# A routed-attention and gated-MLP kernel: a second chunk goes to the 26-product out-projection, and the forms it needs are made earlier

## The chip, the cores and the metric

The kernel runs on one core of a Trainium2 chip. The metric is the device time of one execution in microseconds (us). Each time is one run of the whole program; the kernel before has three.

## What is computed

```python
# routed attention, B=4, H=8, S=768, D=64, 16 centroids per head
mask = q_assign[:, :, :, None] == k_assign[:, :, None, :]
scores = np.where(mask, scale * np.matmul(q, k.transpose(0, 1, 3, 2)), -1e9)
attn_out = np.matmul(softmax(scores), v)
# its heads side by side are x: 3072 tokens x 512
h = x @ w_in                      # 512 -> 2048
g = h * erf(softplus(h))
out = g @ w_out                   # 2048 -> 512
```

All of it is float32. The change concerns only the last product, `g @ w_out`, and what is made for it.

## The kernel before

The attention takes the first 405 us or so and is not touched. Then the 3072 tokens go through the MLP in six chunks of 512 (`NCHUNK`). The 2048 hidden features are two lots of 1024.

**In-projection** (`hidden`, line 727). One call makes one lot of one chunk. It works in four steps of `j`, and in each step multiplies by Strassen's scheme in Winograd's form: seven products of half-size blocks in place of eight. One product there is two matmuls of 128x128 by 128x256; the profile records every float32 matmul as two. A product lands in one of eight PSUM banks (`bank`, line 676, in turn), and VectorE adds it to the results (`fresh`, line 686; ScalarE copies the first of the seven). TensorE can run ahead of these additions until all eight banks are taken.

**Gate** (`gate`, line 741; `gate26`, line 868). ScalarE computes Softplus and Erf, each behind a table load, and VectorE multiplies the outcome into `g`.

**Out-projection.** There are two kinds. Chunks 0 and 1 use `project` (line 779): seven products for each lot and each half of the chunk, so 28 products of four matmuls, 112 matmuls. Chunks 2 to 5 use `project26` (line 921): one scheme of 26 products of four matmuls, 104 matmuls, for both lots at once. The tables `RIGHT`, `LEFT`, `LEFT_STEPS` and `AFTER` (lines 64 to 107) say which sums of `w_out` blocks (right forms) and of `g` blocks (left forms) each product takes, and how VectorE and ScalarE spread the products over the outputs.

**The right forms of the 26-product scheme.** `forms26` (line 832) makes them on GpSimd, once, from the blocks of `w_out`; these lie in memory in the form that `project` uses, so part of that is first turned back. Each step of `FORM_STEPS` (line 55) adds or subtracts two blocks of 128x1024 in two pieces of 128x512. Eight forms stay in SBUF: `slot` (line 812) gives six places in `more_out`, by `HOME`, and two in `w_out`. Ten forms stream: they are stored to DRAM (`b_dram`) and read back in turn into a ring of three buffers (`load_stream`, line 853). Before, 14 pieces are made beside chunk 1's second `project` (line 1260) and 26 beside chunk 2's in-projections (line 1268, through `paired`, line 899); a b12 block of `w_out` that chunk 1's `project` still multiplies by can't be turned back until it has.

**What sets the order.** Instructions on TensorE, VectorE, ScalarE and GpSimd stand in the order in which the Python code issues them (`InOrder`, line 113). Work that belongs to another stage is put in a list, `aside_work`, and `block` (line 708) issues `pace` items of it after each product. The DMAs of the sync engine (SP) are one queue that waits in order. The main loop is at lines 1238 to 1278. The order around the change is:

| stage | before | after |
|---|---|---|
| 1 | chunk 1 in-projection, lot 0 | the same |
| 2 | chunk 0 `project`, lot 1 | the same |
| 3 | chunk 1 in-projection, lot 1 | the same, with the form pieces |
| 4 | chunk 1 `project`, lot 0, then lot 1 | chunk 1 `project26` |
| 5 | chunk 2 in-projections, then `project26` | the same |

All recorded instructions carry line 121 in the profile, that of the helper in `InOrder`, so they are told apart by their tiles. `g`, `osb`, `u` and `x_own` are what they are in the code; `g_more` is the buffer of the left forms in chunks 0 and 1 and the ring after that; `bank` and `turned` are PSUM.

Of the kernel before, what the change touches and what calls it, by code (L numbers as in the profile page):

```python
# [3 lines left out]

# [6 lines left out]
F32 = mybir.dt.float32  # L11
# [9 lines left out]
P = 128  # L21
# [30 lines left out]
FIRST_MASKS = {(2, 0): ("k", 0), (2, 1): ("q", 0), (2, 2): ("k", 1), (5, 2): ("q", 1)}  # L52

KAPPA = {1: (0, 1), 2: (0, 0), 0: (1, 1), 3: (1, 0)}
FORM_STEPS = [
    (0, -2, -8, 1, -1), (10, -4, -8, -1, 7), (9, -5, -6, -1, 3), (1, -3, -5, -1, -1), (2, -6, 1, 1, -1),
    (9, -4, 2, -1, 0), (9, -7, 1, -1, 5), (6, -1, -5, 1, 1), (3, -6, 10, -1, -1), (4, 10, 6, -1, -1),
    (9, 1, 0, -1, 4), (7, -7, -8, -1, 8), (6, -6, 6, -1, -1), (9, -2, 6, 1, 2), (10, -7, 10, 1, 6),
    (5, -7, 0, -1, -1), (9, -1, 5, 1, 9), (7, -3, 10, -1, -1),
]  # L60
EARLY_FORMS = (2, 3, 4, 5, 6, 7)
HOME = (1, 0, 2, 3, 4, 5)
LAG = 1
RIGHT = [
    2, 7, -3, 100, -6, 3, 101, 4, -1, 102, 6, 103, 0,
# [42 lines left out]
DONE = {0: 15, 6: 20, 7: 23, 1: 23, 5: 23, 3: 24, 4: 25, 2: 25}  # L108
N_STREAM = 10
RING = 3  # L110


class InOrder:
# [16 lines left out]
def kernel(  # L130
# [671 lines left out]


    ring, extra = [], []
    b_dram = dram.tile([N_STREAM, P, FG * HM], F32, name="b_dram")

    def w_block(b):
        lot, h = KAPPA[b // 2]
# [9 lines left out]
    def flat(t):  # L818
        return t.rearrange("p f m -> p (f m)")
# [7 lines left out]
            else:  # L827
                extra.append([t[:, i * HM : (i + 1) * HM] for i in range(3)])

    turns26 = itertools.cycle((9, 8))  # L830

    def forms26(early):
        work = []
        for f in (0, 2) if early else (4, 6):
            b12, b22 = w_out[:, f : f + 2, HM:], w_out[:, HF + f : HF + f + 2, HM:]
            work.append(functools.partial(minus_of, b12, b22, b12, ge))
        for n, (o, a, b, sign, k) in enumerate(FORM_STEPS):
            if (n in EARLY_FORMS) != early:
                continue
            o = next(turns26) if o == 9 else o  # L840
            out_, a_, b_ = (slot(x) if x >= 0 else w_block(-1 - x) for x in (o, a, b))
            form = plus_of if sign > 0 else minus_of

            def piece(f, out_=out_, a_=a_, b_=b_, form=form, k=k):
                c = slice(f, f + 2)
                form(out_[:, c], a_[:, c], b_[:, c], ge)
                if f and k >= 0:
                    nc.sync.dma_start(out=b_dram[k].rearrange("p (f m) -> p f m", f=FG), in_=out_)

            work += [functools.partial(piece, f) for f in (0, 2)]  # L850
        return work

    def load_stream(k):
        nc.sync.dma_start(out=flat(ring[k % RING]), in_=b_dram[k % N_STREAM])

    def left26(n, i):
        if i >= 16:
# [37 lines left out]
    def hidden26(n, lot, generation=()):  # L895
        generation = list(generation)
        first_steps = [functools.partial(left_step, n, x) for x, step in enumerate(LEFT_STEPS) if step[0] < 0]

        def paired(work):
            if not generation:  # L900
                return work
            both = []
            for w in work + idle(14 - len(work)):
                g = generation[:1]
                del generation[:1]
                both.append(lambda w=w, g=g: [f() for f in (w, *g)])
            return both

        def middle():
            finish_aside()  # L910
            aside_work.extend(paired(gate_work(n, lot, 0, first_steps if lot else ())))

        if lot:
            aside_work.extend(paired(gate_work(n, 0, 1)))
        else:
            aside_work.extend(paired([]))
        hidden(n, lot, {1: middle})
        finish_aside()
        return generation

    def project26(n):
        for s in range(2):
            osb_of[n, s] = outp.tile([P, 2, DM], F32, name="osb")
        temps = extra[3]

        def c_at(i):
            if i >= 8:
                return temps[i - 8]
            t = i // 2
            return osb_of[n, t // 2][:, t % 2, (i % 2) * HM : (i % 2 + 1) * HM]  # L930

        first_half, second_half, gate_products = gate26(n, 1, 1)
        curves = {-1: first_half[0], 0: first_half[1], 1: second_half[0], 2: second_half[1]}
        gate_products = [gate_products[i] for i in (3, 1, 0, 2)]
        between = right_forms(ve, *x_parts(n + 1)) if n + 1 < NCHUNK else []
        banks26 = {}

        def evict(p):
            m = banks26.pop(p)
            for op, d, src, sign in AFTER[p]:  # L940
                dst = c_at(d)
                source = m if op in "ca" else c_at(src)
                if op in "aA":
                    (plus_of if sign > 0 else minus_of)(dst, dst, source)
                elif op == "C" and p == 4:
                    if sign > 0:
                        ve.tensor_copy(out=dst, in_=source)
                    else:
                        ve.tensor_scalar(out=dst, in0=source, scalar1=-1.0, scalar2=None, op0=ALU.mult)
                elif sign > 0:  # L950
                    ae.copy(out=dst, in_=source)
                else:
                    ae.activation(out=dst, in_=source, func=ACT.Copy, scale=-1.0)
            for t in range(4):
                parts = [DONE[2 * t], DONE[2 * t + 1]]
                o = osb_of[n, t // 2]
                if n + 1 < NCHUNK:
                    if max(parts) == p:
                        nc.sync.dma_start(out=out_v[2 * n + t // 2, :, t % 2], in_=o[:, t % 2])
                else:  # L960
                    for v in range(2):
                        if parts[v] == p:
                            c = slice(v * HM, (v + 1) * HM)
                            nc.sync.dma_start(out=out_v[2 * n + t // 2, :, t % 2, c], in_=o[:, t % 2, c])

        curves[-1]()
        for p, r in enumerate(RIGHT):
            banks26[p] = m = bank()
            lhs = left26(n, LEFT[p])
            g26 = N_STREAM * (n - 2) + r - 100  # L970
            rhs = ring[g26 % RING] if r >= 100 else slot(r) if r >= 0 else w_block(-1 - r)
            for f in range(FG):
                te.matmul(m, lhsT=lhs[:, f], rhs=rhs[:, f], start=(f == 0), stop=(f == FG - 1))
            if r >= 100:
                if g26 + RING < N_STREAM * (NCHUNK - 2):
                    load_stream(g26 + RING)
            for x, step in enumerate(LEFT_STEPS):
                if step[0] == p:
                    left_step(n, x)
            if p < 3:  # L980
                evict(p)
                curves[p]()
            elif p - LAG >= 3:
                evict(p - LAG)
            if p in (4, 5):
                for f in gate_products[(p - 4) * 2 : (p - 4) * 2 + 2]:
                    f()
            if p >= len(RIGHT) - 4 and between:
                between.pop(0)()
            if p == 12:  # L990
                load_x(n + 2)
        for p in sorted(banks26):
            evict(p)
        for s in range(2):
            for lot in range(2):
                del g_of[n, s, lot]
# [244 lines left out]
    aside_work += together(idle(2) + gates(0, 0, (0,)), all_weights(4, N_LATE))  # L1241
    hidden(0, 1, pace=2, first=ve.tensor_copy)
    finish_aside()
    for n in range(2):
        between = right_forms(ve, *x_parts(n + 1)) if n + 1 < NCHUNK else []
        if n == 0:
            aside_work += gates(0, 0, (1,), between) + gates(0, 1, (0,))
        else:
            aside_work += gates(n, 1, (0, 1), between)
        project(n, 0, 2 if n else 3)  # L1250
        finish_aside()
        if n == 0:
            aside_work += together(gates(0, 1, (1,)), idle(2) + [fence] + out_forms[2] + out_forms[3])
            hidden(1, 0, first=ve.tensor_copy)
            finish_aside()
            load_x(2)
            aside_work += gates(1, 0)
        if n == 1:
            take_places(2)
            aside_work += forms26(True)  # L1260
        project(n, 1, 2)
        finish_aside()
        if n == 0:
            hidden(1, 1)
            finish_aside()
            load_x(3)
    take_places(2)
    generation = forms26(False)
    for n in range(2, NCHUNK):
        generation = hidden26(n, 0, generation)  # L1270
        generation = hidden26(n, 1, generation)
        for work in generation:
            work()
        generation = []
        if n == 2:
            for k in range(RING):
                load_stream(k)
        project26(n)


# [30 lines left out]
```

## Time and profile before

| | |
|---|---|
| time, median of 3 runs | 984.88 us (984.54 to 985.0) |
| the profiled execution, its own time | 984.51 us |
| its span from first to last instruction | 982.8 us |
| granted TensorE clock over the span | 0.999 |
| TensorE busy | 971.8 us |
| VectorE busy | 748.5 us |
| GpSimd busy | 404.9 us |
| stores of right forms to DRAM (`b_dram<-g_more`), issue to landing | 2.6 us |
| reads of right forms (`g_more<-b_dram`), issue to landing | 3.3 us |

The profiled execution is 0.37 us shorter than the median, so a difference worked out in the profile is taken off the median as it is. The span leaves out 1.7 us that lie around it. "Busy" of an instruction includes what it waits for after it was handed to its engine, for example for a memory port.

### The profile page before, as it was taken

What the parts mean: (1) busy time and instruction counts of PE and PEld (TensorE: products, weight loads), DVE (VectorE), ACT (ScalarE), POOL (GpSimd) and SP (SyncE); (2) the same over time, 40 slices, a digit from 0 to 9 for tenths busy, and PEclk for the clock granted to TensorE, in tenths of its full rate; (3) what the DMA queues carried; (4) which work ended last, traced back from release to release, by engine and by line L of the source; (5) the groups of instructions that cost most, each with busy time, mean ns of one, the idle gap of its engine ahead of it and who ended that gap; (6) DMA issues with size and microseconds to landing.
All of it is one profiled execution on the core that took longest, in us unless ns stands there. A gap on an engine that the chain in (4) does not pass through costs nothing.

```text
span 982.8 us, 20793 instructions
## 1 busy us (share of the span) xinstructions
PE 971.8 (99%) x8298; PEld 726.6 (74%) x8298; DVE 748.5 (76%) x1417; ACT 518.9 (53%) x771; POOL 404.9 (41%) x277
## 2 busy tenths in 40 slices
PE   8999999999999999999999999999999999999998
PEld 3555555555555555688888888887888888888887
DVE  8888888888888886879767586668666866685766
ACT  3777777777777665486523320552166226413541
POOL 1688887787888888762210079500000000000000
PEclk9999999999999999999999999999999999999999
DMA  9444444444444210232001103413302420141023
GB/s 215 89 110 110 110 109 109 109 109 102 96 109 111 51 35 18 92 105 87 1 0 43 43 26 144 153 65 109 128 0 80 135 86 1 56 138 64 1 86 107
DMA packets 155696, 82.12 MB, mean 84 GB/s; under 512 B 129488, under 2 KB 139728, under 8 KB 155600
## 3 DMA queue, kind: packets, MB, share of 16 engines
q1 hardware_dynamic: 153248, 80.50, 30.2%
q8 instruction: 65, 1.06, 0.5%
q10 hardware_dynamic: 2352, 0.30, 0.2%
q14 instruction: 31, 0.25, 0.1%
HBM read 62.95 MB, written 17.83 MB: 82 GB/s over the span
## 4 chain that ended last, share of the span: by engine, by line
PE 93%; DVE 3%; ACT 2%; issue 1%; DMA 0%; DVEq 0%; ACTq 0%
PE bank L121 40%; PE turned L121 31%; PE sc L121 16%; PE wide L121 6%; ACT a_s L121 1%; DVE g L121 1%; DVE nmx L121 1%; ACT L121 1%; DMA in_q<-in_q_dram 0%; DVE kT L121 0%; DVE g_more L121 0%; DVE sims L121 0%; DVE osb L121 0%; DVE qT L121 0%; ACT osb L121 0%
## 5 line engine op out<-in xcount | busy, mean ns | idle before, releaser
L121 POOL TENSOR_TENSOR more_out<-more_out,pr 128x768 f32<-128x768 f32 x128 | 217.1, 1696 | 18.7 <-ACT pr L121 10.1
L121 DVE TENSOR_REDUCE nmx<-wide 128x2 f32<-128x768 f32 x189 | 180.5, 955 | 48.2 <-PE wide L121 47.2
L121 ACT ACTIVATE pr<-sc 128x768 f32<-128x768 f32 x192 | 148.9, 812 | 94.2 <-PE wide L121 78.6
L121 PE MATMUL turned<-pr,in_v 128*32 128x194 f32 x3072 | 145.5, 330 | 0.0
L121 DVE TENSOR_TENSOR g<-bank,g 128x256 f32<-128x256 f32 x222 | 89.6, 420 | 60.3 <-PE bank L121 36.9
L121 PEld LDWEIGHTS turned<-pr,in_v 128*32 128x32 f32 x3072 | 91.5, 109 | 51.2 <-issue 21.3
L121 PE MATMUL bank<-x_own,w_in 128*128 128x256 f32 x424 | 104.5, 380 | 0.0
L121 PE MATMUL sc<-qT,kT 64*128 64x384 f32 x528 | 98.3, 486 | 0.0
L121 DVE TENSOR_TENSOR g<-g 128x512 f32<-128x512 f32 x96 | 66.8, 696 | 30.7 <-PE bank L121 20.9
L121 PEld LDWEIGHTS bank<-x_own,w_in 128*128 128x128 f32 x424 | 80.3, 190 | 11.6 <-issue 0.6
L121 ACT ACT_TABLE_LOAD x48 | 61.6, 1283 | 44.6 <-DVE g L121 43.9
L121 PE MATMUL bank<-w_out,g 128*128 128x256 f32 x352 | 81.2, 379 | 0.0
L121 DVE TENSOR_TENSOR g<-a_s,g 128x512 f32<-128x512 f32 x96 | 72.2, 769 | 5.4 <-ACT a_s L121 5.4
L121 PE MATMUL bank<-x_more,more_in 128*128 128x256 f32 x296 | 76.0, 379 | 0.0
L121 PEld LDWEIGHTS bank<-w_out,g 128*128 128x128 f32 x352 | 66.9, 190 | 9.1
L121 POOL TENSOR_TENSOR more_out<-pr,pr 128x768 f32<-128x768 f32 x32 | 60.2, 1882 | 27.9 <-ACT pr L121 27.9
L121 PEld LDWEIGHTS <-qv 64*128 64x128 bf16 x384 | 27.0, 93 | 52.8 <-issue 36.6
L121 PEld LDWEIGHTS sc<-qT,kT 64*128 64x128 f32 x528 | 50.0, 187 | 21.2 <-ACT inv L121 2.3
L121 PE MATMUL wide<-kv,qv 64*128 64x384 bf16 x378 | 64.1, 328 | 1.3 <-DVE nmx L121 0.6
L121 PE MATMUL wide<-km,qm 64*128 64x384 bf16 (+1 forms) x378 | 62.6, 327 | 0.0
L121 PEld LDWEIGHTS bank<-x_more,more_in 128*128 128x128 f32 x296 | 56.2, 190 | 7.7
L121 ACT COPY g<-bank 128x256 f32<-128x256 f32 x28 | 10.2, 365 | 92.2 <-PE bank L121 87.4
(195 smaller groups left out, 1790.0 us busy)
## 6 DMA issues: line engine op xcount, KB each, us to landing
g_more<-b_dram SPq DMA_DIRECT2D x40, 512.0 KB, 3.3
x_own<-in_moe_w_in_dram SPq DMA_DIRECT2D x13, 512.0 KB, 4.4
in_v<-in_v_dram SPq DMA_DIRECT2D x32, 192.0 KB, 3.1
x_dram<-more_out SPq DMA_DIRECT2D x128, 48.0 KB, 2.0
x_own<-x_dram SPq DMA_DIRECT2D x6, 1024.0 KB, 5.2
in_k<-in_k_dram SPq DMA_DIRECT2D x59, 96.0 KB, 2.8
in_q<-in_q_dram SPq DMA_DIRECT2D x58, 96.0 KB, 2.8
out_dram<-osb SPq DMA_DIRECT2D x20, 256.0 KB, 2.7
```

What stands on the lines that cost most here:

```text
L121: ins = getattr(self.engine, name)(*args, **kw)
```

## The change

Chunk 1 goes through `hidden26` (its lot 1) and `project26` as chunks 2 to 5 do. So `forms26` has to be finished one and a half stages earlier, while chunk 0's second `project` still uses `w_out` and `more_out` in their old form. The 18 steps and two turnings become 20 steps in two tables, again 40 pieces of 128x512. The 24 pieces of `EARLY_FORMS` touch only places that chunk 0's lot 0 has left; the 16 of `LATE_FORMS` write places of lot 1. `HOME` is permuted for this. A form that an in-place turning would have given is held in a spare buffer (`HELD`, the ends of two ring tiles). Two resident forms, slots 0 and 5, go to DRAM and are read back once their places are free (`KEPT`, `load_kept`). Two of the first three streamed forms are already in their ring buffers, so only one is read before `project26` (`load_stream(1)`, after the last piece). The gates of chunk 1's lot 0 are both issued beside chunk 0's second `project`, whose `pace` goes from 2 to 3, and no left forms of Strassen's kind are made for chunk 1. The load of chunk 3's `x` and the right forms of chunk 2's `x` move into chunk 1's `project26`.

```diff
-HOME = (1, 0, 2, 3, 4, 5)
+EARLY_FORMS = [
+    (-6, -4, -6, -1, None), (11, -2, -8, -1, None), (1, -3, -5, -1, None), (2, -6, 1, 1, None),
+    (0, -4, 11, -1, 7), (8, -7, 11, -1, 8), (9, -5, -6, -1, 3), (11, -2, 11, 1, 10),
+    (8, -7, 11, -1, 11), (6, -1, -5, 1, 1), (9, -1, 8, 1, 9), (8, 1, 11, -1, 4),
+]
+LATE_FORMS = [
+    (3, -6, 0, -1, None), (4, 0, 6, -1, None), (0, -7, 0, 1, 6), (7, -3, 0, -1, None),
+    (10, -4, 2, -1, 0), (6, -6, 6, -1, None), (9, -2, 6, 1, 2), (8, -7, 1, -1, 5),
+]
+HOME = (4, 0, 2, 3, 1, 5)
+KEPT = {0: 10, 5: 11}
+HELD = 11
...
+    def place26(x, f):
+        if x == HELD:
+            return extra[f // 2].rearrange("p j t -> p (j t)").rearrange("p (f m) -> p f m", f=2)
+        return (slot(x) if x >= 0 else w_block(-1 - x))[:, f : f + 2]
...
+    def load_kept(i):
+        nc.sync.dma_start(out=slot(i), in_=b_dram[KEPT[i]].rearrange("p (f m) -> p f m", f=FG))
...
-        nc.sync.dma_start(out=flat(ring[k % RING]), in_=b_dram[k % N_STREAM])
+        nc.sync.dma_start(out=flat(ring[(k + 2) % RING]), in_=b_dram[k % N_STREAM])
...
-    for n in range(2):
...
-        if n == 1:
-            take_places(2)
-            aside_work += forms26(True)
-        project(n, 1, 2)
...
-    generation = forms26(False)
-    for n in range(2, NCHUNK):
...
+    aside_work += together(gates(0, 1, (1,)), idle(2) + [fence] + out_forms[2] + out_forms[3])
+    take_places(2)
+    hidden(1, 0, first=ve.tensor_copy)
+    finish_aside()
+    load_x(2)
+    making = forms26(EARLY_FORMS)
+    for work in making[:8]:
+        work()
+    del making[:8]
+    aside_work += together(gate_work(1, 0, 0) + gate_work(1, 0, 1), making)
+    project(0, 1, 3)
+    finish_aside()
+    take_places(2)
+    making = forms26(LATE_FORMS)
+    making.insert(2, functools.partial(load_kept, 5))
+    making.append(functools.partial(load_kept, 0))
+    making.append(functools.partial(load_stream, 1))
+    for n in range(1, NCHUNK):
+        if n > 1:
+            hidden26(n, 0)
+        hidden26(n, 1, making if n == 1 else ())
+        project26(n)
```

## The prediction

> **What bounds the kernel now.** First the page: busy shares, and the chain that ended last by engine.
>
> ```profile
> PE 971.8 (99%) x8298; PEld 726.6 (74%) x8298; DVE 748.5 (76%) x1417; ACT 518.9 (53%) x771; POOL 404.9 (41%) x277
> PE 93%; DVE 3%; ACT 2%; issue 1%; DMA 0%; DVEq 0%; ACTq 0%
> ```
>
> TensorE is the bound, so a matmul less is time less, unless TensorE stops somewhere. In the chain in order of time, 10.36 us of TensorE hold 48 matmul records: 0.2158 each, so 0.4316 for one float32 matmul. Where it stops is read from stages. TensorE's timeline gives their borders; the table of windows gives busy time and records by engine, in the order TensorE, weight loads, VectorE, ScalarE, GpSimd.
>
> ```profile
> 602.20:626.40 24.20, 24.20 (x113) 21.29 (x113) 12.66 (x25) 7.95 (x10) 24.20 (x21) 1.00 0.34 131
> 626.40:651.10 24.70, 24.62 (x114) 21.01 (x113) 17.99 (x37) 13.80 (x15) 2.36 (x2) 1.00 0.25 86
> 651.10:698.70 47.60, 45.36 (x209) 39.35 (x208) 37.88 (x79) 15.65 (x32) 0.00 (x0) 1.00 0.39 128
> 698.70:722.90 24.20, 24.20 (x114) 21.30 (x113) 13.65 (x34) 7.95 (x10) 0.00 (x0) 1.00 0.16 55
> 722.90:747.05 24.15, 24.15 (x113) 21.26 (x112) 16.97 (x41) 14.41 (x16) 0.00 (x0) 1.00 0.00 1
> 747.05:791.95 44.90, 44.90 (x210) 39.52 (x208) 34.28 (x72) 15.14 (x30) 0.00 (x0) 1.00 0.42 135
> ```
>
> The first three lines are chunk 2's two in-projections and its 26 products, the others chunk 3's. 104 matmuls are 104 x 0.4316 = 44.89 us, and chunk 3 needs no more; chunk 2 takes 47.62, 2.73 over. Its in-projections take 48.86 where 112 matmuls are 48.34: 0.52 over. All other stages from 408 us on are at their number, and about 4.2 us follow the last matmul. The only 3.25 us that TensorE loses are in chunk 2, the one with GpSimd beside it. VectorE's timeline shows why (start, us, operation):
>
> ```profile
> 578.02 2.77 DVE L121 TENSOR_TENSOR g<-a_s,g 128x512 f32<-128x512 f32 x2
> 581.04 1.42 DVE L121 TENSOR_TENSOR g_more<-g 128x512 f32<-128x512 f32 x1
> ...
> 623.54 5.76 DVE L121 TENSOR_TENSOR g<-a_s,g 128x512 f32<-128x512 f32 x1
> ...
> 629.56 0.68 DVE L121 TENSOR_TENSOR g<-a_s,g 128x512 f32<-128x512 f32 x1
> ```
>
> And GpSimd's:
>
> ```profile
> 578.52 3.39 POOL L121 TENSOR_TENSOR more_out<-w_out 128x512 f32<-128x512 f32 x2
> ...
> 623.80 2.50 POOL L121 TENSOR_TENSOR g_more<-w_out,more_out 128x512 f32<-128x512 f32 x2
> 626.25 2.51 POOL L121 TENSOR_TENSOR w_out<-w_out,g_more 128x512 f32<-128x512 f32 x2
> ```
>
> A VectorE addition from SBUF alone takes 0.68 us free and on average 1.38 beside GpSimd (nine from 573.35 to 585.74), while additions from PSUM stay at 0.42. GpSimd's pieces follow each other 1.23 us apart when free and 1.68 when VectorE comes between. One VectorE operation, at 623.54, waited through four pieces until GpSimd had none left. VectorE then never caught up within the stage: ScalarE's table load ahead of the products starts 5.74 us into chunk 2's product stage (656.83) and 1.37 into chunk 3's (748.42). Of these 4.37 us of lag TensorE lost 2.73: 1.64 are free.
>
> **What the Trainium skill says.** "SBUF — State Buffer", section Who interferes with whom: a VectorE instruction with two SBUF inputs shares a read port with a GpSimd instruction that reads SBUF; the second to issue waits for the first. The trace agrees with 1.38 against 0.68, and PSUM additions untouched. It differs at 623.54, where the wait outlasted several GpSimd instructions. "ScalarE: Activation LUTs", section What ACT_TABLE_LOAD costs: about 1283 ns; the trace has 1283 in the mean.
>
> **The change part by part.** *Fewer products.* The order of TensorE's instructions has 8 matmuls less: 112 become 104. 8 x 0.4316 = **-3.45**.
>
> *Chunk 2 loses its company.* No GpSimd piece is left after chunk 1, so chunk 2 runs as chunk 3 does: **-3.25**, unless chunk 1 hands a lag on.
>
> *GpSimd's 40 pieces move.* The last old form ends at 494.40 (493.12 + 1.28), and the early 24 follow at once; their places are free since 481. They meet 8 VectorE operations at the end of chunk 1's lot 0, and 8 gate products and 6 half-size additions beside chunk 0's second `project`: 24 x 1.23 + 16 x 0.45 + 6 x 0.22 = 38.0, to 532.4. By then the late pieces' places are free (that `project` ends at 529.7). Late: 16 x 1.23 + 7 x 0.45 = 22.9, to **555.3**. Chunk 1's 26 products start at 529.7 + 24.17 = 553.9, each 1.73 long. The last form is used as product 13; the one on the longest way is stream 1 for product 6: after the last piece its buffer is stored (2.6) and read anew (3.3), to 561.3, and product 6 starts at 553.9 + 6 x 1.726 = 564.3. Margin 3.0, so nothing; were every piece contended, 494.4 + 40 x 1.68 = 561.6, and 3.3 late.
>
> *VectorE beside them, up to 529.7.* Its 8 operations in chunk 1's lot 0 cost 8 x 0.70 = 5.6 more in a window of 12.0 us where it was busy 9.75: some 3.4 late, and eight banks let TensorE run seven products (6.0 us) ahead: nothing. Beside `project` the contention costs 8 x 0.70 + 6 x 0.6 = 9.2, and eight Strassen sums of 0.6 no longer needed give back 4.8; seven products are 12.1 us ahead there. At the end the second gate's products wait for ScalarE: first products done about 522.5, two loads and four curves of 1.05 make 529.3, four contended products 5.5 and the additions between them about 1: VectorE reaches the next stage at 536. TensorE needs its second bank again at 537.5. Bounds 0 to 1.5 (products at 1.75, as the worst of 575.68); I take **+0.3**. A gain is excluded: TensorE loses nothing there now.
>
> *Chunk 1's lot 1 and products.* Late pieces meet three left forms (about 544, absorbed: VectorE needs 17 of 24 us) and four gate products within the last 4.4 us, which can't be: 4 x 0.70 = 2.8. The gate's table load then comes 1.37 + 2.8 = 4.2 into the product stage; less 1.37 and the free 1.64: **+1.2**. Bounds: 0 if the pieces have thinned out; 7 x 0.70 - 1.64 = 3.3 if nothing is absorbed.
>
> *DMAs and SP.* Two stores and two reads of kept forms are added and two ring reads drop out, on SP, which waits in order: chunk 0's last two output stores now stand behind form stores and the read into slot 5, till about 540. Who needs them is `osb`, reused at 555; nothing waits. The load of chunk 3's x moves to about 575 and is used after 690. Both cost nothing; if a store came 15 us later, that would show at once.
>
> Sum: -3.45 - 3.25 + 0.3 + 1.2 = -5.2. The profiled execution, 984.51 (span 982.8, and 1.7 around it), becomes 979.3; the median, 0.37 above it, 984.88 - 5.2 = **979.7**.
>
> **The rivals.** *The stall only moves* (0.18): chunk 1 pays what chunk 2 paid, 3.25, so 984.88 - 3.45 = 981.4, up to 982.9. For it: the same pieces meet the same kind of gate products. Against: the 5.76 us wait came once among some sixteen meetings.
>
> *Forms late* (0.10): contended throughout, stream 1 is 3.3 late, with the other terms 979.7 + 3.3 = 983.0. Against: GpSimd took 1.23 wherever VectorE was on PSUM.
>
> *GpSimd keeps the port* (0.20, slower): the wait at 623.54 followed 18 free pieces and ended with GpSimd's work. In chunk 1's lot 0 VectorE's first meeting, at 496.6, comes after ten free pieces (from 484.28), with some 22 ahead and no wait for TensorE until about 523.9 (494.4 + 24 x 1.23). Frozen so long, 27.3, less the 6.0 ahead, TensorE loses 21.3: 984.88 - 5.2 + 21.3 = 1001. It decides from 5.2 + 6.0 = 11.2 us of freezing, nine pieces. Against: in fifteen other meetings VectorE got in after at most one piece.
>
> That the matmuls don't get fewer is excluded by the instructions' order.
>
> **How the numbers follow.** Forecast 979.7, chance 0.52, its own range 978.2 (no stall at all: 984.88 - 6.7) to 981.5. Range 978.0 to 984.0: with it come the moved stall and late forms; about 0.2 is left out, the slow case. A measurement of this kernel tells 0.2% (2 us) from no change: faster means under 982.9. Forecast, moved stall and a part of late forms: 0.70; within 0.11; slower 0.19.
>
> **What would show it.** Right: chunks 2 to 5 each 48.3 and 44.9; chunk 1's products 45 to 48; GpSimd done near 555 with no gap over 1 us; VectorE's SBUF additions 1.0 to 1.8 from 496 to 553, none over 3. Wrong: one over 10 us, TensorE idle on a ring buffer at product 6, or a product stage of chunk 1 over 49.

## The result and the profile after

The median went from 984.90 us (six runs, 984.54 to 985.00) to **978.82 us** (six runs, 978.31 to 979.01): 6.08 us less, ratio 0.9938 with a 95% interval of 0.9925 to 0.9951. The forecast was 979.7. The profiled execution took 978.7, with a span of 976.8.

The first two lines of the page after, busy shares and the chain of waits by engine (the helper that issues all instructions is at line 124 in the kernel after and its variants):

```profile
PE 968.1 (99%) x8282; PEld 724.4 (74%) x8282; DVE 757.9 (78%) x1431; ACT 526.8 (54%) x799; POOL 409.9 (42%) x277
PE 97%; DVE 1%; SPq 1%; issue 0%; DMA 0%; ACT 0%; DVEq 0%
```

TensorE has 16 records less, which is 8 float32 matmuls. Its share of the chain rose from 93 to 97%: what it used to wait for is gone. The table of windows, with borders from TensorE's timeline (TensorE busy, weight loads, VectorE, ScalarE and GpSimd, each with its records; then granted clock, DMA share, GB/s): chunk 1's second in-projection, its 26 products, chunk 2's two in-projections, its 26 products.

```profile
530.05:554.22 24.17, 24.17 (x113) 21.28 (x112) 21.27 (x34) 8.81 (x11) 24.04 (x17) 1.00 0.43 157
554.22:599.16 44.94, 44.94 (x209) 39.44 (x208) 35.92 (x75) 15.04 (x30) 0.00 (x0) 1.00 0.51 170
599.16:623.33 24.17, 24.17 (x113) 21.28 (x112) 13.63 (x34) 7.95 (x10) 0.00 (x0) 1.00 0.17 54
623.33:647.51 24.18, 24.18 (x114) 21.28 (x112) 17.00 (x41) 14.41 (x16) 0.00 (x0) 1.00 0.00 1
647.51:692.40 44.89, 44.89 (x209) 39.52 (x208) 34.27 (x72) 15.13 (x30) 0.00 (x0) 1.00 0.42 135
```

The 47.62 us of chunk 2's products are now 44.89, and its in-projections 48.35 instead of 48.86: it runs as chunk 3 does. Chunk 1's products, which now have GpSimd's work ahead of them, take 44.94, 0.05 over the number of their matmuls. All 40 of GpSimd's pieces lie between 494.70 and 554.09, one directly after the other: from the end of chunk 1's first in-projection, beside chunk 0's second `project`, to the end of the second in-projection.

VectorE's timeline shows its additions from SBUF among those pieces (start, us, operation):

```profile
496.92 0.82 DVE L124 TENSOR_TENSOR g<-a_s,g 128x512 f32<-128x512 f32 x1
498.98 1.66 DVE L124 TENSOR_TENSOR g<-a_s,g 128x512 f32<-128x512 f32 x1
...
551.37 1.59 DVE L124 TENSOR_TENSOR g<-a_s,g 128x512 f32<-128x512 f32 x1
...
553.22 1.42 DVE L124 TENSOR_TENSOR g<-a_s,g 128x512 f32<-128x512 f32 x1
...
555.22 0.67 DVE L124 TENSOR_TENSOR g<-a_s,g 128x512 f32<-128x512 f32 x1
...
556.15 0.67 DVE L124 TENSOR_TENSOR g<-a_s,g 128x512 f32<-128x512 f32 x1
```

No operation comes near the 5.76 us of before: from 496 to 554 they took 0.68 to 1.76 us. Of the second gate's four products two were contended; the other two fell after GpSimd's last piece and took 0.67. GpSimd's timeline has that last pair of pieces:

```profile
548.22 2.96 POOL L124 TENSOR_TENSOR g_more<-w_out 128x512 f32<-128x512 f32 x2
551.15 2.94 POOL L124 TENSOR_TENSOR g_more<-w_out,more_out 128x512 f32<-128x512 f32 x2
```

ScalarE's timeline has the table load that measures VectorE's lag, 3.02 us into the product stage (557.24 - 554.22), where chunk 2 of before had 5.74:

```profile
557.24 1.28 ACT L124 ACT_TABLE_LOAD   x1 [6.77 <-DVE g L124]
```

And the chain of waits in order of time stays on TensorE across product 6, which starts at about 564.6; stream 1 had landed at 560.50:

```profile
556.11 3.45 PE turned L124 x16
559.57 10.36 PE bank L124 x48
569.93 3.50 PE turned L124 x16
```

### The profile page after: what moved, and what is told of

It reads as the page before. It is cut to its first block, busy times and chain, and to the rows that moved or that the text cites. A ratio compares the mean times of both kernels' runs of the same rounds, so it can differ in the third digit from the quotient of the medians.

```text
span 976.8 us, 20838 instructions
## 1 busy us (share of the span) xinstructions
PE 968.1 (99%) x8282; PEld 724.4 (74%) x8282; DVE 757.9 (78%) x1431; ACT 526.8 (54%) x799; POOL 409.9 (42%) x277
## 4 chain that ended last, share of the span: by engine, by line
PE 97%; DVE 1%; SPq 1%; issue 0%; DMA 0%; ACT 0%; DVEq 0%
PE bank L124 43%; PE turned L124 31%; PE sc L124 17%; PE wide L124 6%; SPq L124 1%; DVE nmx L124 1%; DMA in_q<-in_q_dram 0%; DVE kT L124 0%; DVE qT L124 0%; DVE km L124 0%; DVE turned L124 0%; DVE sims L124 0%; ACT qm L124 0%; DVE g_more L124 0%; DVE osb L124 0%
## 5 line engine op out<-in xcount | busy, mean ns | idle before, releaser
L124 DVE TENSOR_TENSOR g<-g 128x512 f32<-128x512 f32 x114 | 78.8, 692 | 42.3 <-PE bank L124 32.2
L124 PE MATMUL bank<-w_out,g 128*128 128x256 f32 x328 | 75.7, 379 | 0.0
L124 PE MATMUL bank<-g_more,g 128*128 128x256 f32 x296 | 69.9, 379 | 0.0
L124 PEld LDWEIGHTS bank<-w_out,g 128*128 128x128 f32 x328 | 62.3, 190 | 8.5
L124 PEld LDWEIGHTS bank<-g_more,g 128*128 128x128 f32 x296 | 56.2, 190 | 7.6
```

The lines of the kernel that those rows point to most:

```text
L124: ins = getattr(self.engine, name)(*args, **kw)
```

## The experiments

Two theories stood against each other. The first is the prediction's: the gain is 8 matmuls less, and the loss of chunk 2 that came from GpSimd beside it. The rival: the loss of chunk 2 has another cause (its place among the stages, its data), and chunk 1 pays something for GpSimd's work that another gain covers.

**GpSimd's late pieces in the kernel before made short.** Fourteen of the 26 pieces beside chunk 2 add 16 elements a partition instead of 512, so that GpSimd is done early; the rest of those right forms isn't computed.

```
-            def piece(f, out_=out_, a_=a_, b_=b_, form=form, k=k):
-                c = slice(f, f + 2)
-                form(out_[:, c], a_[:, c], b_[:, c], ge)
+            def piece(f, o=o, out_=out_, a_=a_, b_=b_, form=form, k=k):
+                c, m = slice(f, f + 2), HM if early or o >= 8 else 8
+                form(out_[:, c, 0:m], a_[:, c, 0:m], b_[:, c, 0:m], ge)
```

> The kernel before, in which 14 of GpSimd's 26 pieces beside chunk 2's in-projections (those that write resident forms, not the streamed ones) add 16 columns in place of 512, so these resident forms are left mostly unmade. GpSimd is then done before VectorE's gate product at 623.5 asks for the port. Theory (chunk 2's 3.25 us come from that one wait for the shared port): chunk 2 takes 48.3 and 44.9 us as chunk 3 does, the time is 984.9 - 3.25 = 981.65, within 0.3. Rival (the loss belongs to the stage: the first reads into the ring, the gate's chain on ScalarE, the output stores): the stage still loses 2.7 to 3.3 us and the time stays at 984.9.

Measured: 981.60 us (five runs, 981.34 to 981.83), ratio 0.9966 (0.9953 to 0.9978). Its table of windows, chunk 2's in-projections and products:

```profile
602.58:626.75 24.17, 24.17 (x113) 21.28 (x112) 12.67 (x31) 7.95 (x10) 11.81 (x20) 1.00 0.59 218
626.75:650.92 24.17, 24.17 (x113) 21.28 (x112) 16.99 (x41) 14.41 (x16) 0.00 (x0) 1.00 0.00 0
650.92:695.82 44.90, 44.90 (x210) 39.52 (x209) 34.28 (x72) 15.13 (x30) 0.00 (x0) 1.00 0.42 135
```

GpSimd is busy for 11.81 of the first window's 24.17 us instead of all of it, and both losses are gone. 984.90 - 981.60 = 3.30 us is what GpSimd's company cost chunk 2. The chunk's place and its gate are the same as before; only the values in the right forms differ. The single additions further down take most of the loss away with all forms made in full. The rival's first half falls.

**The same in the kernel after.** Twenty of the 40 pieces add 16 elements a partition; the rest of those forms isn't computed.

```
-                form(place26(o, f), place26(a, f), place26(b, f), ge)
+                m = HM if o >= 8 else 8
+                form(*(place26(x, f)[:, :, 0:m] for x in (o, a, b)), ge)
```

> The changed kernel, in which the 20 of GpSimd's 40 pieces that write resident forms add 16 columns in place of 512 (these forms are left mostly unmade); GpSimd is done long before chunk 1's products. Theory (what is left of the contention is covered: ScalarE's table load comes 3.0 us into chunk 1's product stage in place of 1.4, and all but 0.05 of that is free): the table load moves to about 1.4 us, the time stays at 978.8, within 0.2. Rival (the predicted +1.5 us of stalls is hidden elsewhere in the span, for example in the start of chunk 1's lot 1): 0.5 to 1.5 us faster, 977.3 to 978.3.

Measured: 978.89 us (five runs, 978.64 to 978.90), ratio 0.9938 (0.9926 to 0.9950), the same as the kernel after. Chunk 1's products take 44.89, and the table load comes 1.36 into them, as in an undisturbed chunk (the table of windows, then ScalarE's timeline):

```profile
554.46:599.35 44.89, 44.89 (x209) 39.52 (x208) 34.27 (x72) 15.13 (x30) 0.00 (x0) 1.00 0.42 135
555.82 1.28 ACT L124 ACT_TABLE_LOAD   x1 [5.12 <-DVE g L124]
```

So what is left of the contention in the changed kernel, 3.02 - 1.36 = 1.66 us of VectorE's lag, costs 0.05 us in the stage (44.94 against 44.89) and nothing that the time shows: the rival's second half falls too.

**The eight matmuls put back.** Products 14 and 15 of chunk 1 run twice.

```
-            for f in range(FG):
-                te.matmul(m, lhsT=lhs[:, f], rhs=rhs[:, f], start=(f == 0), stop=(f == FG - 1))
+            for _ in range(2 if n == 1 and p in (14, 15) else 1):
+                for f in range(FG):
+                    te.matmul(m, lhsT=lhs[:, f], rhs=rhs[:, f], start=(f == 0), stop=(f == FG - 1))
```

> The changed kernel with products 14 and 15 of chunk 1's 26 multiplied twice into the same bank: 8 float32 matmuls more, nothing else. Theory (TensorE is the bound through the whole stage, each matmul is worth 0.4316 us): 978.8 + 3.45 = 982.3, within 0.2. Rival (part of the 3.45 is taken back by VectorE, which has more to do in a 26-product stage than in two Strassen stages and could be what sets its length): TensorE's extra work is partly hidden, under 981.5.

Measured: 982.23 us (eight runs, 981.92 to 982.45), ratio 0.9972 (0.9962 to 0.9983). 982.23 - 978.82 = 3.41 for 8 matmuls; the stage grew from 44.94 to 48.41.

**Two pieces more in the kernel after.** The first late piece is made three times instead of once, so that GpSimd ends near where the prediction had it.

```
     making = forms26(LATE_FORMS)
+    for _ in range(2):
+        making[0]()
```

> The changed kernel with the first late piece made three times: GpSimd ends 2.5 to 3.4 us later, at 556.6 to 557.5, so all four gate products at the end of chunk 1's lot 1 meet it in place of two. Stream 1 lands at 563 to 564, still ahead of product 6 at 564.6: no wait there. Theory (the stage has 1.65 us of lag free behind a table load at +1.36, and beyond that TensorE pays one for one): the load comes at +4.1 to +4.6, as the prediction had it, TensorE loses 1.1 to 1.6 us, the time is 979.9 to 980.4. If instead the forms' way decides, two pieces are free and the time stays at 978.8.

Measured: 979.92 us (five runs, 979.73 to 980.16), ratio 0.9950 (0.9936 to 0.9964). GpSimd ends at 557.7, and all four gate products meet it (1.61, 1.42, 1.09 and 1.42 us). The table load, by ScalarE's timeline, comes at 558.66, 4.19 into the stage:

```profile
558.66 1.28 ACT L124 ACT_TABLE_LOAD   x1 [7.95 <-DVE g L124]
```

The stage takes 46.12, 1.23 over, and the list of waits gives most of that to the wait for a gated activation:

```profile
PE turned L124 <- DVE g L124: 1.0, 1, 1.0
```

This is, to a tenth, the case that the prediction took as the likeliest: lag 4.2, loss 1.2. What keeps the kernel after from it is how early GpSimd was done: 0.13 us ahead of the product stage (554.09 against 554.22), where it is 3.2 us into it here.

**Eight pieces more.** The same edit with `range(8)`.

> The changed kernel with the first late piece made nine times, so GpSimd has 8 pieces more to do ahead of the late forms: 8 x 1.23 to 1.68 = 10 to 13 us, its end at 564 to 567 in place of 554.1. Theory (the forms' way is a second bound, 4.1 us behind TensorE: stream 1 landed at 560.5 and product 6 starts at 564.6): stream 1 lands at 570 to 574, TensorE waits 6 to 9 us ahead of product 6, 984.8 to 987.8. Rival (GpSimd's end is covered by the ring and the resident forms, and the forecast of late forms overrated it): under 1 us slower.

Measured: 991.37 us (four runs, 990.23 to 991.88), ratio 1.0063 (1.0046 to 1.0080). Stream 1 lands at 574.68. The list of waits:

```profile
PE bank L124 <- DMA g_more<-b_dram: 9.8, 1, 9.8
```

So the form on the longest way is late where it was said to be, ahead of product 6. The wait, 9.8 us, is 0.8 above the expected range, and the time is 3.6 above it. The windows from the stop on show where the rest comes from (the eighth column is the granted clock):

```profile
565.00:574.80 9.80, 0.05 (x1) 0.02 (x1) 8.82 (x14) 1.32 (x4) 2.99 (x2) 0.78 0.72 259
574.80:580.70 5.90, 5.89 (x14) 4.73 (x15) 0.00 (x0) 1.08 (x3) 0.00 (x0) 0.50 0.65 250
580.70:590.00 9.30, 9.30 (x44) 8.19 (x44) 4.75 (x10) 1.16 (x3) 0.00 (x0) 1.00 0.29 93
```

After 9.8 us without a matmul, TensorE's clock is at 0.50 for another 5.9 us: 14 records of about 427 ns where 216 is the rule, 14 x 0.211 = 3.0 us more. The Trainium skill says this ("TensorE: Matmul & The Clock Gate", section What's actually happening: after an idle window of about 3.4 us the clock falls to half, until it has been busy for such a window); the trace agrees on the half, with 5.9 us from the restart until it was back. A shorter stop can be enough, as the next variant shows.

**When is VectorE shut out?** The rival that ends slower, GpSimd keeping the port, rested on a single wait. Five variants of the kernel before place VectorE operations elsewhere beside the same pieces. A free piece is one at 1.23 us, with no VectorE operation on two SBUF inputs beside it; the counts of free pieces below take in the one that is running when VectorE asks. First, the gate's products three steps earlier:

```
-        return [lambda: run([f() for f in soft + erf]), *also, *idle(8 - len(also)), *products_of]
+        return [lambda: run([f() for f in soft + erf]), *also, *idle((5 if (n, lot, half) == (2, 0, 0) else 8) - len(also)), *products_of]
```

> The kernel before, with the four gate products of chunk 2's lot 0 (first half) issued three TensorE products earlier on VectorE. They then ask for the port at about 621.5, when ScalarE has the curves ready, after some 16 free pieces of GpSimd and with six ahead. If a long run of free pieces is what lets GpSimd keep the port, the wait lasts to GpSimd's end at 628.8 again, now some 7 us, chunk 2 loses 4 to 5 us in place of 3.25, and the time is 985.5 to 987. If it was chance of the moment (or needs that very pair of operands), VectorE gets in after one piece, waits about 0.7 for each of the four, chunk 2 loses under 1 us and the time is 981.7 to 982.5.

Measured: 985.81 us (twelve runs, 985.33 to 985.96), ratio 1.0008 (1.0000 to 1.0017). VectorE's timeline:

```profile
621.91 8.45 DVE L121 TENSOR_TENSOR g<-a_s,g 128x512 f32<-128x512 f32 x2 [0.49 <-ACT a_s L121]
```

The first of these two took 7.85 us, until GpSimd was done. It asked 2.1 us earlier in the stage than in the kernel before, after 17 free pieces, and took 2.1 us longer. The in-projections lose 4.05 us (52.39), the products 0.07 (44.96; table load 3.09 into them). TensorE stopped for 2.0 us, and soon after the restart its clock was at 0.50 for 3.41 us:

```profile
632.25:635.66 3.41, 3.41 (x10) 2.68 (x9) 2.99 (x9) 1.49 (x2) 0.00 (x0) 0.50 0.53 190
```

The stop is shorter than the idle window of about 3.4 us that the same page gives (it is cited above), so the measurement decides: here 2.0 us were enough.

Next, seven small VectorE additions of two SBUF inputs (128 x 256, their sum used by nothing) all along chunk 2's first in-projection:

```
+    def small_add():
+        t = up.tile([P, HM], F32, name="u")
+        ve.tensor_tensor(out=t, in0=w_in[:, 0, 0:HM], in1=w_in[:, 1, 0:HM], op=ALU.add)
+
+    def adds(at, n):
+        return [small_add if i in at else (lambda: None) for i in range(n)]
...
-            aside_work.extend(paired(gate_work(n, lot, 0, first_steps if lot else ())))
+            aside_work.extend(paired(gate_work(n, lot, 0, first_steps if lot else adds((1, 4, 7), 8) if n == 2 else ())))
...
-            aside_work.extend(paired([]))
+            aside_work.extend(paired(adds((2, 5, 8, 11), 14) if n == 2 else []))
```

> The kernel before, with seven additions of 128x256 from SBUF to a spare buffer put on VectorE along chunk 2's lot 0 (after TensorE's products 2, 5, 8, 11, 15, 18 and 21 of 28), so that GpSimd never runs more than three or four pieces without meeting VectorE. If it takes a long free run of GpSimd for VectorE to be kept out, all seven and the gate products at 623.5 get in after at most one piece (0.7 to 1.8 us each), chunk 2 loses under 0.5 us and the time is 981.7 to 982.3, though VectorE has more to do. If the wait belongs to those operands or that place in the stage, the product at 623.5 waits 5 us again, and the time is 984.9 to 985.5.

Measured: 983.37 us (twenty runs, 983.03 to 983.51), ratio 0.9984 (0.9978 to 0.9991). Each addition took 0.4 to 1.5 us, and so did the gate's products after them, 1.09 to 1.42 each. The in-projections are at 48.35; the products still lose 1.62 (46.51), since GpSimd, delayed by the additions, was still there for all four gate products and the table load came 4.64 into the stage. The expectation had the mechanism and missed that rest.

Then one such addition alone, at three places, after 8, 11 and 15 free pieces as it turned out. The first two with `adds((8,), 14)` and `adds((13,), 14)` in the second of those calls, the third with `adds((3,), 8)` in the first.

> The same with the addition at about 610 us, after some seven free pieces. If seven is long enough: a wait of 19 us to GpSimd's end, TensorE loses about 13, 994 to 996. If it is let in (a run of up to five was in the changed kernel), the product at 623.5 comes after a run of eleven, and waits 5 us again if that is long: 984.9; else 981.7 to 982.3.

> The kernel before, with one such addition, about 614.5 us, after some ten free pieces of GpSimd. If a run of ten is long enough, it waits until GpSimd's end at 628.8, 14 us, TensorE runs out of banks after 6 of them, and the time is 989 to 991. If it is let in, the gate product at 623.5 meets GpSimd after a run of seven, and tells whether that is long: 5 us again and 984.9, or under 2 us and 981.7 to 982.3.

> The kernel before with one addition on VectorE at about 618 us, after some 13 free pieces of GpSimd; so far runs up to 11 let VectorE in, and runs of 16 and 18 kept it out. If 13 is still short: the addition gets in, the gate products follow within four pieces and get in too, about 982.2. If it is long enough: a wait of some 10 us to GpSimd's end, TensorE stops for 4 to 5 in the in-projections, and a part of the lag is left for the product stage: 986 to 989.

Measured, one run each: 982.16, 982.19 and 987.16 us; 23 runs of the kernel before lie within 0.7 us, so that single runs tell these apart. VectorE's timelines of the first two show the addition let in at once, or after one piece:

```profile
611.04 1.24 DVE L121 TENSOR_TENSOR u<-w_in 128x256 f32<-128x256 f32 x1
```

```profile
615.35 0.68 DVE L121 TENSOR_TENSOR u<-w_in 128x256 f32<-128x256 f32 x1
...
624.04 1.05 DVE L121 TENSOR_TENSOR g<-a_s,g 128x512 f32<-128x512 f32 x1
...
625.35 1.42 DVE L121 TENSOR_TENSOR g<-a_s,g 128x512 f32<-128x512 f32 x1
```

That of the third:

```profile
619.74 9.52 DVE L121 TENSOR_TENSOR u<-w_in 128x256 f32<-128x256 f32 x1
629.18 0.41 DVE L121 TENSOR_TENSOR g<-bank,g 128x256 f32<-128x256 f32 x1
```

An operation of 0.4 us took 9.52 us, and everything behind it in VectorE's order waited with it; the next addition, from PSUM, could only start at 629.18. GpSimd's timeline ran on through the wait at its free pace, up to its last pair:

```profile
601.93 2.49 POOL L121 TENSOR_TENSOR g_more<-w_out 128x512 f32<-128x512 f32 x2
...
626.50 2.48 POOL L121 TENSOR_TENSOR w_out<-w_out,g_more 128x512 f32<-128x512 f32 x2
```

It stopped TensorE for 3.7 us, whose clock fell here too, with 8 records at about 427 ns afterwards; the third addition cost the in-projections 5.67 us (54.01). So the same addition, four pieces apart, gains 2.7 us or loses 2.3. In all these traces VectorE got in after a run of up to 11 free pieces (11 x 1.23 = 13.5 us) and was shut out until GpSimd's queue was empty after 15 or more (18 in the kernel before, 17 with earlier products, 15 here); between 11 and 15 nothing was measured. In the kernel after the longest run is about 10, up to 496.92, not five as the expectation had it. The two additions at 617.96 and 620.76 among the seven got in, with the same operands at nearly the same time as the one that didn't: it is the run before it, not the place, that goes with the wait. Nor is it the moment within a GpSimd piece: VectorE was shut out when it asked 0.10, 0.60 and 0.97 us after a piece's start, and let in at 0.31 (the first addition) and 0.88 (the second). Nor is it how little GpSimd has left: the gate product at 624.04, four pieces before the end, got in. Why a long run does this was not found.

**The end of the kernel.** By the profiles the time after the last matmul's start is 4.55 us in all variants of the kernel before and 4.93 to 4.95 in the variants of the kernel after above; the difference lies between the last transfer's landing and the end of the span, 1.02 against 1.41. The DMAs take eight semaphores in turn, and the theory was that it matters which of them carries the last one. Small transfers on SP's queue shift that:

```
     load_x(2)
+    pad = dram.tile([3, P, 1], F32, name="pad")
+    for i in range(3):
+        nc.sync.dma_start(out=pad[i], in_=alleps)
```

> The changed kernel with three DMAs of 128x1 to a spare DRAM buffer put on SP about 507 us, nothing else. From the last DMA's landing to the end of the span the kernel before needs 1.02 us and the changed one 1.41; so do all variants of each. DMAs take eight semaphores in turn, SP's closing waits go through these in a fixed order, and the change brings 13 DMAs more, so the last DMA has another semaphore. Theory: three more bring it back to the one it had before, the end takes 1.0 us and the time is 0.35 to 0.4 lower, 978.4 to 978.5. Rival (the longer end comes from something else in the changed program): 978.8.

> The same with six, so that the last DMA has the semaphore waited for last. Theory: the other closing waits, some 0.065 us each, are over when it lands; the end takes 0.8 to 0.9 us, the time is 978.2 to 978.4. Rival: 978.8.

Measured: 979.28 us with three (five runs, 978.99 to 981.94), ratio 0.9948 (0.9936 to 0.9960), and 978.95 with six (five runs, 978.64 to 979.51), ratio 0.9940 (0.9926 to 0.9953). The stretch from the last landing to the end came out as expected, 1.03 us with three and 0.84 with six. By the traces the last transfer has the semaphore that SP's closing waits come to first in the kernel after, second in the kernel before and with three, last with six. So its place among these waits does go with the length of the end; one wait of 0.065 more explains only a part of the 0.39 between before and after, and the rest is open.

The time didn't fall, and the theory's rival is not confirmed by that, because the edit did more than it was meant to. The transfers didn't go out at about 507 us but in the middle of the attention, as SP's timelines with three and with six show:

```profile
53.78 1.38 SPq L1260 DMA_DIRECT2D pad<-alleps  x3
53.34 2.80 SPq L1260 DMA_DIRECT2D pad<-alleps  x6
```

In both traces TensorE falls behind the kernel after at 65 to 67 us, by 3.7 us with three and 1.2 with six, and the attention ends at 411.49 and 409.08 instead of 408.42. With three the last transfer also landed later after the last matmul, so that from there to the end it is 5.00 us, against 4.34 with six. That the transfers delayed the loads behind them on the queue fits this and wasn't tried. What a shorter end is worth in time stays open.

## Why the prediction was right

Each term of the sum, against what the runs showed (three steps on the way are 0.1 off as written: 22.8, 561.2 and 3.2 late are right; nothing hangs on them):

- *Fewer products, -3.45.* Measured 3.41 by putting them back. Right.
- *Chunk 2 loses its company, -3.25.* Measured 3.30 by taking GpSimd out of the kernel before, and chunks 2 to 5 are each at 48.35 and 44.89. Right, the cause too.
- *Start of chunk 1's lot 1, +0.3.* The stage is at 24.17, so nothing. The term was inside its bounds and too careful.
- *Chunk 1's lot 1 and products, +1.2.* Measured 0.05. The step that was mis-sized is the end of GpSimd's work: 1.4 us into the product stage in the sum (555.3 against 553.9), 0.13 ahead of it in the trace (554.09 against 554.22). The sum let 23 full-size VectorE operations delay GpSimd by 0.45 each; in the trace three of them took 0.67 or 0.68 and met no delay, the last two gate products among them, and 3 x 0.45 is most of the difference. So the lag was 1.66 instead of 2.8, and 1.64 had been put down as free. That the mechanism is the one described is shown by two pieces more, which give the predicted lag and loss.
- *Forms' way to product 6, margin 3.0.* 4.1 in the trace, since GpSimd was early. With 8 pieces more the wait comes at the named place; the margin was real and finite.
- *Not foreseen, +0.38:* the end of the kernel, where the last transfer has another semaphore.

The two terms that carry the change were right by their mechanism. That the total is only 0.9 us from the forecast is in part luck: two terms were together 1.45 too high, and 0.38 that nobody foresaw went the other way. The measured terms make -3.41 - 3.30 + 0.05 + 0.38 = -6.28, against -6.08 for the medians; the 0.20 between them is not explained. In the two profiled executions -5.81 is to be explained: there the attention, which the change doesn't touch, ended 0.43 later after than before (408.42 and 407.99; 408.3 or more in the profiles of the other variants of before), and -6.28 + 0.43 = -5.85.

How lag becomes loss can be read off the profiles. Where the table load came 3.0 us or less into a product stage, TensorE lost at most 0.05; beyond that it lost 2.72 at 5.74, 1.62 at 4.64, 1.23 at 4.19, 0.47 at 3.49, 0.44 at 3.45 and 0.07 at 3.09. That is one for one past 3.02, which is 1.65 more than an undisturbed chunk's 1.37: the prediction's free 1.64, found there from a single stage, holds in five others.

Of the rivals, *the stall only moves* is wrong for this kernel: no addition from SBUF takes over 1.8 us. *Forms late* names the right place, but not the right amount. *GpSimd keeps the port* describes something real, three times seen, and its price was not exaggerated (9.52 us for one 0.4 us addition); what the prediction could only argue, that VectorE gets in after ten free pieces, was right and decided the outcome. Five pieces more ahead of 496.9 without a VectorE addition from SBUF would have made a run of 15, which shut VectorE out in the kernel before; that wasn't tried in the kernel after.

## What to carry to other kernels

Move side work to where its consumers have slack, and count the slack in the lag of the engine that it disturbs: here 1.65 us are free, and every us beyond is a us of TensorE. Beside a long series of GpSimd additions from SBUF, let VectorE come between at least every ten: one addition of 0.4 us, put in after 8 or 11 pieces, gave the kernel before 2.7 us, and put in after 15 it cost 2.3. Before adding to a transfer's way, work out its margin at the consumer, because a TensorE that stopped for 2.0 us or more here paid again in its clock.

## What was not expected of the hardware

- The shut-out. The Trainium skill ("SBUF — State Buffer", section Who interferes with whom) has the second instruction wait for the first; that is what most meetings show (0.68 us becoming 1.38). After 15 or more free GpSimd pieces the wait lasted until GpSimd had nothing left: operations of 0.4 to 0.7 us took 5.76, 7.85 and 9.52 us.
- The clock after a stop: 2.0 us without a matmul were followed by 7 records at 427 ns, 3.7 us by 8, 9.8 us by 14. In the kernel before, gaps of 1.63 and 1.37 us between the starts of two matmuls left the clock at 1.00.
- The closing of the kernel, from the last landing on, was 1.02 us in one program and 1.41 in another with the same last transfers, and 1.03 and 0.84 when small transfers shifted the last one's semaphore.
